# Attention pieces in one written-out sequence instead of ready lists with a table of priorities

## The chip, the cores and the metric

The kernel runs on one core of a Trainium2 chip. The metric is the device time of one execution in microseconds (us), the median of several runs. TensorE (PE) does the matmuls and the transposes; VectorE (DVE), ScalarE (ACT) and GpSimd (POOL) work on whole tiles; SyncE (SP) starts most of the transfers.

## What is computed

Sixteen heads of attention (2 batches, 8 heads, 1152 positions, 64 numbers each), in which neighbouring queries are averaged first, feed two MLPs, one behind the other.

```python
q_pool = q.reshape(B, H, S // 2, 2, D).mean(axis=3)
scores = scale * np.matmul(q_pool, k.transpose(0, 1, 3, 2))
scores = scores - np.max(scores, axis=-1, keepdims=True)
attn = np.exp(scores)
attn = attn / (np.sum(attn, axis=-1, keepdims=True) + 1e-09)
x = np.matmul(attn, v)
...
g = x @ w_gate
silu = g * (1.0 / (1.0 + np.exp(-g)))
x = (silu * (x @ w_val)) @ w_out
...
h = x @ w_in
g = np.maximum(h, 0.0) + alpha * np.minimum(h, 0.0)
out = g @ w_out
```

Between attention and the first MLP (512 to 1536 to 512) the heads are put side by side, 1152 rows of 512 numbers; the second MLP is 512 to 2048 to 512. All inputs are fp32. The kernel keeps each factor of a product as a high and a low part and multiplies three times: high by high, high by low, low by high.

## The kernel before

The kernel is written as a **plan**. Each step is one call of `add`: the engine (or two to choose from, the second in `also`), a duration from a formula for its size, what it reads and writes, the buffers and PSUM banks that it holds, and a function that writes its instructions. `plan.run` (called in L1128) puts the 2222 steps in one sequence, `plan.emit` writes their instructions in that sequence, and each engine executes its own in order. So the sequence sets the order on every engine, and with it who waits for whom.

**What sets the order.** `run` plays the kernel through as a list of events. Each engine has a ready list, sorted by priorities from the table `KNOB`: one set of numbers each for scores, minima, exponentials, transposes, evacuations and V blocks (`qk`, `mn`, `exp`, `t`, `ev`, `v`), with other sets for the first and the last pair. PE's list has two surcharges, `stay` for a step of another tile shape and `alt` for a change between scores and transposes. A step is bound to a free slot of its buffers' classes; PSUM has eight banks. While PE has nothing to do early in the plan, `run` inserts small filling matmuls (`idle`, L354). The durations (`mm`, `act`, `dve`, `gp`) are formulas of the size; a table load of ACT is in none of them.

**Attention** goes by eight pairs of heads, p0 to p7, each of 576 averaged queries: four units of 128 for both heads (`two`) and one corner of the last 64 of either head (`corner`).
- Scores: a unit is cut into three runs of 384 keys, six matmuls a cut (L719); the corner has nine matmuls in all (L738). For the first two units of p0 they are made of unsplit fp32 queries ("raw"). The sums of neighbouring queries are L662 on DVE; the queries of a whole pair are summed and split by L648 and L649 on POOL and L650 on DVE, and for the corner by L678 on POOL.
- DVE reads each cut from its bank and carries the running minimum on (L687 the first cut, L689 the others).
- ACT makes the exponentials of 1152 numbers a row and their sum (L693).
- PE transposes them, sixteen blocks at a time (L762), and the last column of blocks apart, four or two at a time (L776). ACT (L752) or DVE (L753) moves the result out of PSUM.
- V blocks (L795): the first 256 queries of a pair are one block, the other 320 a second one, each of 36 matmuls in the trace.
- The inverses of the sums go through a POOL, a DVE, a PE (L809) and an ACT step (L812) and transfers, and `finish` multiplies by them.

**The MLPs.** A third of the tokens has plain products: `contract` (L894), twelve matmuls of 384 columns. The others go by seven products in place of eight (L906, six matmuls each; DVE adds their results in L912). The Silu of the gate is L962 on ACT, its product with the value L967 on DVE. L1037 and L1071 are the second matrices of the MLPs. The weights come as 64-bit words, of which ACT (L504), DVE (L505 to L507) and POOL or DVE (L523, L524) make fp32; the high part is then split off on ACT or POOL (L485, L486), the low part on DVE or POOL (L477, L478). The MLP's bank class `b` may take four of the eight banks while attention still runs. The first plain products of the gate need tokens of the first four pairs alone, so they may stand among the steps of the last pair.

## Time and profile before

| | us |
|---|---|
| median of 3 runs | 604.35 (604.27 to 604.91) |
| the profiled execution | 604.31 |
| its span, first to last instruction | 602.5 |
| PE busy | 597.4 |
| DVE busy | 521.9 |
| ACT busy | 363.7 |
| POOL busy | 171.0 |

The profile is of one execution. The ends of PE's matmuls are modelled, so a short wait can hide in its busy time; distances between the starts of groups show it. PEld is the load of the stationary tile, and PE's waits are booked there with their releasers. A line is that of a step's instruction, so L693 is every exponential of every pair. In time, attention lasts to about 197 us, and the MLPs take the rest.

### The profile page before, as it was taken

The numbers are of one execution on the slowest core, as the hardware profiler recorded it, in microseconds if no ns is written. First come the engines' busy times: TensorE is split into PE (matmuls) and PEld (weight loads), VectorE is DVE, ScalarE is ACT, GpSimd is POOL, SyncE is SP. The second block draws the span as 40 slices with busy tenths as digits, with TensorE's granted clock in tenths as the row PEclk, the third lists the DMA queues.
The fourth block names the chain that finished last, engine by engine and source line by source line (L and its number), as shares of the span: only waits on it lengthen the run. The fifth ranks groups of instructions, "written<-read, shape, count | busy, mean of one in ns | idle before, by whom it ended". The sixth has DMA issues, their size and how long they took to land.

```text
span 602.5 us, 12214 instructions
## 1 busy us (share of the span) xinstructions
PE 597.4 (99%) x4762; PEld 532.7 (88%) x4762; DVE 521.9 (87%) x1059; ACT 363.7 (60%) x616; POOL 171.0 (28%) x187
## 2 busy tenths in 40 slices
PE   8999999999999999999999999999999999999997
PEld 5877877877877999999999999999999989989986
DVE  6998898899989899999589999889999999988552
ACT  6898888978999655555346434446575654544320
POOL 4663433523275222113320210456110300230000
PEclk9999999999999999999999999999999999999999
DMA  6342331330321313243303223121212313110012
GB/s 208 109 140 66 115 101 61 120 101 22 112 92 29 133 70 140 71 154 133 133 1 139 98 112 141 71 71 70 71 70 96 132 54 140 70 71 1 0 62 97
DMA packets 17914, 55.36 MB, mean 92 GB/s; under 512 B 2808, under 2 KB 4288, under 8 KB 17856
## 3 DMA queue, kind: packets, MB, share of 16 engines
q1 hardware_dynamic: 17568, 54.19, 25.7%
q8 instruction: 37, 0.61, 0.4%
q10 hardware_dynamic: 288, 0.39, 0.2%
q14 instruction: 21, 0.17, 0.1%
HBM read 52.17 MB, written 2.40 MB: 91 GB/s over the span
## 4 chain that ended last, share of the span: by engine, by line
PE 95%; DVE 2%; ACT 1%; issue 1%; POOL 0%; DVEq 0%; ACTq 0%
PE bank L906 24%; PE bank L1071 16%; PE bank L894 14%; PE bank L1037 12%; PE bank L795 11%; PE bank L719 8%; PE bank L762 5%; PE bank L738 2%; PE bank L776 1%; ACT wide L693 1%; DVE wide L689 1%; PE bank L354 1%; DVE wide L687 0%; DVE magnitudes L506 0%; PE bank L809 0%
## 5 line engine op out<-in xcount | busy, mean ns | idle before, releaser
L906 PE MATMUL bank<-fed,weights 128*128 128x384 f32 x600 | 114.2, 336 | 0.0
L523 POOL TENSOR_TENSOR magnitudes<-magnitudes 128x256 f32<-128x256 f32 x61 | 52.3, 873 | 217.1 <-DVE magnitudes L507 176.4
L906 PEld LDWEIGHTS bank<-fed,weights 128*128 128x128 f32 x600 | 105.6, 188 | 0.7 <-DVE plain L912 0.2
L1071 PE MATMUL bank<-wide,turned 128*128 128x512 f32 (+1 forms) x444 | 101.8, 384 | 0.0
L1071 PEld LDWEIGHTS bank<-wide,turned 128*128 128x128 f32 x444 | 81.6, 188 | 15.4
L693 ACT ACTIVATE wide<-wide,stats 128x1152 f32<-128x1152 f32 x63 | 78.8, 1252 | 21.2 <-DVE wide L689 20.9
L894 PE MATMUL bank<-x,weights 128*128 128x384 f32 x480 | 88.6, 337 | 0.0
L894 PEld LDWEIGHTS bank<-x,weights 128*128 128x128 f32 x480 | 83.8, 188 | 1.6 <-issue 0.7
L1037 PE MATMUL bank<-turned,wide 128*128 128x384 f32 x432 | 76.6, 334 | 0.0
L1037 PEld LDWEIGHTS bank<-turned,wide 128*128 128x128 f32 x432 | 75.1, 188 | 0.0
L689 DVE TENSOR_SCALAR_CACHE_REDUCE wide<-bank,stats 128x384 f32<-128x384 f32 x126 | 72.6, 613 | 1.0
L795 PE MATMUL bank<-turned,plain 128*64 128x320 f32 (+1 forms) x576 | 73.4, 409 | 0.0
L912 DVE TENSOR_TENSOR plain<-bank,plain 128x384 f32<-128x384 f32 x100 | 55.0, 550 | 13.0 <-PE bank L906 11.6
L795 PEld LDWEIGHTS bank<-turned,plain 128*64 128x64 f32 x576 | 39.9, 137 | 29.3 <-issue 2.5
L752 ACT ACTIVATE turned<-bank 128x512 f32<-128x512 f32 (+2 forms) x120 | 58.3, 555 | 4.7 <-PE bank L762 2.1
L719 PE MATMUL bank<-fed 64*128 64x384 f32 x540 | 58.0, 348 | 0.3 <-ACT plain L812 0.2
L477 DVE TENSOR_TENSOR weights<-magnitudes,weights 128x1024 fp32r<-128x1024 f32 x37 | 45.8, 1255 | 4.7 <-POOL weights L486 3.4
L906 PE MATMUL bank<-early,weights 128*128 128x384 f32 x240 | 48.5, 336 | 0.0
L719 PEld LDWEIGHTS bank<-fed 64*128 64x128 f32 x540 | 45.7, 186 | 1.4 <-ACT plain L812 0.5
L485 ACT ACTIVATE weights<-magnitudes 128x1024 fp32r<-128x1024 f32 x32 | 33.8, 1056 | 20.2 <-DVE magnitudes L507 10.4
L504 ACT ACTIVATE magnitudes<-plain 128x1024 f32<-128x1024 f32 x32 | 36.5, 1143 | 10.9 <-DVE weights L477 5.6
L953 ACT ACTIVATE turned<-plain,signs 128x384 fp32r<-128x384 f32 x48 | 28.5, 615 | 23.7 <-DVE plain L1007 23.6
(101 smaller groups left out, 877.0 us busy)
## 6 DMA issues: line engine op xcount, KB each, us to landing
plain<-in_w_out SPq DMA_DIRECT2D x28, 512.0 KB, 4.2
plain<-in_w_in SPq DMA_DIRECT2D x16, 512.0 KB, 3.2
plain<-in_w_gate SPq DMA_DIRECT2D x10, 512.0 KB, 3.3
plain<-in_w_val SPq DMA_DIRECT2D x10, 512.0 KB
plain<-in_vt SPq DMA_DIRECT2D x8, 576.0 KB, 5.3
plain<-in_qt SPq DMA_DIRECT2D x7, 576.0 KB, 3.7
plain<-in_kt SPq DMA_DIRECT2D x7, 576.0 KB, 3.6
out<-plain SPq DMA_DIRECT2D x8, 256.0 KB, 3.2
```

The costliest lines, as they stand in the source:

```text
L477: ways = [(DVE, dve(w), lambda: nc.vector.tensor_tensor(dst(), src(), hi().bitcast(F32), ALU.subtract), True), (POOL, gp2(w), lambda: nc.g ...
L523: ways = [(POOL, gp2(2 * P), lambda a=a, b=b, op=op, n=n: nc.gpsimd.tensor_tensor(U(n), a(), b(), op), True), (DVE, dve(2 * P), lambda a=a ...
L689: go = lambda: nc.vector.tensor_scalar(e.ap[:, js], src(), scale, m(i - 1), ALU.mult, ALU.min, accum_out=m(i))
L693: add(ACT, act(S, True, True), lambda: nc.scalar.activation(e.ap, e.ap, AF.Exp, bias=st.ap[:, 2:3], scale=-1.0, accum_out=x.sums.ap[:, n:n ...
L719: nc.tensor.matmul(s[j].ap[:, :CUT], l(half), r(half, js), start=a == 0, stop=a == len(terms) - 1)
L752: ACT, act(cols), lambda: nc.scalar.activation(to(), src(), AF.Copy), at + turn("ev", p, n), ts, [key], ts + [et],
L795: nc.tensor.matmul(acc.ap[half, :n], x.vn.ap[:, (j * NK + kc) * D:(j * NK + kc) * D + D], b.ap[:, (j * NK + kc) * n:(j * NK + kc) * n + n] ...
L894: nc.tensor.matmul(acc.ap[:, :TB], l, x0[:, r, c], start=c == 0 and a == 0, stop=c == KC - 1 and a == 2)
L906: nc.tensor.matmul(bank_.ap[:, :TB], l, seven(xb, k, c, r), start=first and c == 0 and n == 0, stop=c == 1 and n == 2, skip_group_check=no ...
L912: add(DVE, dve(TB), lambda: nc.vector.tensor_tensor(dst.ap, a.ap[:, :TB], b.ap, ALU.add), prio, [a] + ([b] if b is not dst else []), [dst] ...
L1037: nc.tensor.matmul(acc.ap[:, :TB], l[:, os_], r, start=n == 0 and m == 0, stop=n == len(g) - 1 and m == 2)
L1071: nc.tensor.matmul(acc.ap[:, :width], l, r[:, cols], start=n == 0 and m == 0, stop=n == len(g) - 1 and m == 2)
```

## The change

`run` no longer chooses. It takes a list of codes, `ORDER` (twice a step's number, plus one for its second engine), and places one step after the other as the list has them. The formulas are left for the choice of banks and buffers and for the number of filling matmuls. `_spot`, `_bind` and `room` go as methods, the numbers in `KNOB` are others, and in the kernel's function all lines move by 10 (L352 is L362). The diff, cut to its core; `ORDER` has 2222 codes, and one row of it is shown:

```diff
-KNOB = dict(hold_pe=0.0251, hold_act=0.2853, hold_dve=0.2093, hold_pool=13.0018, stay=9.7412, ramp=-6.5151, last=-0.69, 
...
+KNOB = dict(hold_pe=0.0169, hold_act=0.2895, hold_dve=0.1806, hold_pool=26.6713, stay=25.5753, ramp=-6.5151, last=-0.69, 
...
+ORDER = """
+8 20 10 48 50 24 12 54 34 14 39 52 26 56 60 16 22 40 18 28 30 98 62 66 58 64 86 68 88 90 42 92 70 72 94 82 84 76 32 154 44 100 46 96 36 74 79 130 102 132
...
+    def run(self, codes):
+
+        free = {PE: self.first, ACT: 0.0, DVE: 0.0, POOL: 1.7, SP: 0.6}
+        moved, port = 2.15, 0.0
+        mode, turned, valued = "rows", False, False
+        owner, binds, order = {}, {}, []
+        before = {}
+        for t in self.tasks:
+            for a in t.after:
+                before.setdefault(a, []).append(t)
+
+        def room(s, at):
+            gone = [owner[c] for c in s.cells if c in owner]
+            if any(b.users for b in gone) or any(self.classes[o]["open"] for o in s.after):
+                return None
+            until = max([b.until for b in gone], default=0.0)
+            return (0, -until) if until <= at else (1, until)
+
+        for code in codes:
+            t = self.tasks[code // 2]
+            w = t.way = t.ways[code % 2]
+            e = w.eng
+            ready = 0.0
+            for d in before.get(t, ()):
+                f = d.way.eng
+                ready = max(ready, d.done + (0.0 if f == e == PE and not d.extra else 0.216 if f == e == DVE else self.LAT[f] + (0.05 if f == POOL != e else 0.0)))
+            idle = [i for i in range(8) if ("ps", i) not in owner or (not owner["ps", i].users and owner["ps", i].until <= free[PE])]
+            at = max(free[e], ready)
+            for i, b in enumerate(t.bufs):
+                if b.slot is None:
+                    spots = [(room(s, at), k, s) for k, s in enumerate(self.classes[b.cls]["slots"])]
+                    _, _, b.slot = min(x[:2] + (x[2],) for x in spots if x[0] is not None)
+                    ready = max([ready] + [owner[c].until for c in b.slot.cells if c in owner])
+                    for c in b.slot.cells:
+                        owner[c] = b
+                    cells = sorted(c[1] for c in b.slot.cells if c[0] == "ps")
+                    if cells:
+                        binds.setdefault(t, []).extend((c, b.cls in "vmb" or (j == 1 if len(cells) == 2 else i == 1)) for j, c in enumerate(cells))
+            start = max(free[e], ready, port if w.port and e == DVE else 0.0)
+            end = start + w.dur
+            if e == PE:
+                if mode == "rows" and not valued and idle:
+                    order += [idle] * int((start - free[e]) / 0.058)
+                if start > free[e] + 1e-6:
+                    end += self.STALL
+                if t.mode != mode:
+                    end += self.TURN[mode, t.mode]
+                    mode = t.mode
+                if mode == "rows":
+                    end += 0.05 if turned and t.kind == "s" else 0.0
+                    turned = t.kind == "t"
+                valued = valued or mode == "cols"
+            if w.port:
+                end = port = max(start, port) + w.dur
+            free[e] = end
+            t.start, t.done = start, end + t.late
+            if t.extra:
+                moved = max(start + 1.25, moved) + t.extra
+                t.done = moved + 0.85
+            for b in t.bufs:
+                b.until = max(b.until, t.done + self.LAT[e])
+                b.users -= 1
+                if not b.users:
+                    self.classes[b.cls]["open"] -= 1
+            order.append(t)
+        self.end = max(t.done for t in self.tasks)
+        self.order = []
+        top = [False] * 8
+        for k in reversed(order):
+            if isinstance(k, list):
+                able = [i for i in k if top[i]]
+                if able:
+                    self.order.append(lambda i=able[-1]: self.idle(i))
+            self.order.append(k.way.emit)
+            for i, low in binds.get(k, ()):
+        self.order.reverse()
...
-    plan.run({PE: K["hold_pe"], ACT: K["hold_act"], DVE: K["hold_dve"], POOL: K["hold_pool"], SP: 0.0}, K["stay"], K["alt"])
+    plan.run([int(c) for c in ORDER.split()])
```

In the program PE has 5 filling matmuls of 128 columns where it had 35; its other matmuls are the same ones. 94 steps are on another engine: two of the first splits of keys go from ACT and DVE to POOL, some ten evacuations net from DVE to ACT, three weight splits from ACT to POOL. ACT has six table loads where it had two. The order differs most at the start and in the last two pairs; PE's last 176 groups are the same in both.

**The start, DVE.** Before, from its first instruction (`bank` is PSUM, `wide` the scores of a unit, `fed` the split queries and keys, `stats` the minima):

```order
L429 MEMSET plain 128x256
L662 TENSOR_TENSOR plain<-plain 128x128
L642 TENSOR_TENSOR fed<-plain,fed 128x384
L687 TENSOR_SCALAR wide_133,stats<-bank 128x384
L689 TENSOR_SCALAR wide_133,stats<-bank,stats 128x384
L687 TENSOR_SCALAR wide_133,stats<-bank 128x384
L689 TENSOR_SCALAR wide_133,stats<-bank,stats 128x384
L662 TENSOR_TENSOR plain<-plain 128x128
L689 TENSOR_SCALAR wide_133,stats<-bank,stats 128x384 x2
L687 TENSOR_SCALAR wide_133,stats<-bank 128x384 x2
L689 TENSOR_SCALAR wide_133,stats<-bank,stats 128x384
L650 SCALAR_TENSOR_TENSOR fed<-plain,fed 128x576
```

After, from its first instruction:

```order
L439 MEMSET plain 128x256
L672 TENSOR_TENSOR plain<-plain 128x128
L697 TENSOR_SCALAR wide_120,stats<-bank 128x384 x2
L699 TENSOR_SCALAR wide_120,stats<-bank,stats 128x384
L672 TENSOR_TENSOR plain<-plain 128x128
L699 TENSOR_SCALAR wide_120,stats<-bank,stats 128x384 x3
L697 TENSOR_SCALAR wide_120,stats<-bank 128x384 x2
L699 TENSOR_SCALAR wide_120,stats<-bank,stats 128x384
L660 SCALAR_TENSOR_TENSOR fed<-plain,fed 128x576
L699 TENSOR_SCALAR wide_120,stats<-bank,stats 128x384 x2
```

The second sum of queries (L662, now L672) stands behind three minima and not four, the split of keys (L642) is gone from here, and the split of queries (L650, now L660) stands behind nine minima as before.

**The start, PE.** Before, from the last raw scores (`plain` at L719) to the first V block:

```order
L719 MATMUL bank<-plain 128x384 x4
L762 MATMUL bank<-plain,wide_133 128x64 x16
L719 MATMUL bank<-plain 128x384 x2
L762 MATMUL bank<-plain,wide_133 128x64 x16
L776 MATMUL bank<-plain,wide_133 128x64 x4
L738 MATMUL bank<-fed 128x384 x9
L762 MATMUL bank<-plain,wide_133 128x64 x16
L719 MATMUL bank<-fed 128x384 x6
L762 MATMUL bank<-plain,wide_133 128x64 x16
L776 MATMUL bank<-plain,wide_133 128x64 x4
L719 MATMUL bank<-fed 128x384 x30
L795 MATMUL bank<-turned_207,plain 64x256 x18
```

After, to the first V block; ahead of it stand twelve raw scores in a row, sixteen transposes, four of the last column and two filling matmuls:

```order
L772 MATMUL bank<-plain,wide_120 128x64 x16
L729 MATMUL bank<-fed 128x384 x6
L748 MATMUL bank<-fed 128x384 x9
L772 MATMUL bank<-plain,wide_120 128x64 x16
L729 MATMUL bank<-fed 128x384 x6
L772 MATMUL bank<-plain,wide_120 128x64 x16
L729 MATMUL bank<-fed 128x384 x6
L786 MATMUL bank<-plain,wide_120 128x64 x4
L729 MATMUL bank<-fed 128x384 x18
L805 MATMUL bank<-turned_170,plain 64x256 x18
```

Six split scores stand ahead of the corner, and the 30 scores ahead of the V block are parted by transposes.

**Pair 7, ACT.** Before, the last exponentials (L693) and the first Silu (L962):

```order
L693 ACTIVATE plain,allsums<-plain,stats 128x1152
L485 ACTIVATE fed<-plain 128x384
L693 ACTIVATE wide_133,allsums<-wide_133,stats 128x1152 x2
L752 ACTIVATE turned_207<-bank 128x8x64 x2
L752 ACTIVATE turned_207<-bank 128x2x2x64
L798 ACTIVATE plain<-bank 128x256
L752 ACTIVATE turned_207<-bank 128x8x64
L812 ACTIVATE plain<-bank 9x128
L752 ACTIVATE turned_207<-bank 128x8x64 x2
L485 ACTIVATE weights_2710<-magnitudes 128x1024
L962 ACT_TABLE_LOAD
L962 ACTIVATE plain<-bank 128x384
```

After, behind the first two exponentials of pair 7:

```order
L972 ACT_TABLE_LOAD
L972 ACTIVATE plain<-bank 128x384
L703 ACT_TABLE_LOAD
L703 ACTIVATE plain,allsums<-plain,stats 128x1152
L762 ACTIVATE turned_170<-bank 128x8x64
L703 ACTIVATE wide_120,allsums<-wide_120,stats 128x1152
L972 ACT_TABLE_LOAD
L972 ACTIVATE plain<-bank 128x384
L762 ACTIVATE turned_170<-bank 128x8x64
L762 ACTIVATE turned_170<-bank 128x2x2x64
L762 ACTIVATE turned_170<-bank 128x8x64 x5
L703 ACT_TABLE_LOAD
```

Two Silus (now L972) stand between exponentials (now L703), and each change of function has a table load ahead of it.

**Pair 7, PE.** Before, from the V block of pair 7's first 256 queries:

```order
L795 MATMUL bank<-turned_207,plain 64x256 x18
L776 MATMUL bank<-plain,wide_133 128x64 x2
L776 MATMUL bank<-plain 128x64 x2
L762 MATMUL bank<-plain,wide_133 128x64 x16
L762 MATMUL bank<-plain 128x64 x16
L776 MATMUL bank<-plain,wide_133 128x64 x4
L762 MATMUL bank<-plain,wide_133 128x64 x32
L809 MATMUL bank<-plain 128x64 x2
L894 MATMUL bank<-x_67,weights_2710 128x384 x12
L795 MATMUL bank<-turned_207,plain 64x320 x18
L894 MATMUL bank<-x_67,weights_2710 128x384 x36
```

After, inside pair 7 (L904 is the gate's plain product, L729, L748, L772 and L786 are scores, corner, transposes and last-column transposes); behind it come 30 scores, then the V block of 320 queries of pair 6 and that of 256 of pair 7 in a row:

```order
L904 MATMUL bank<-x_67,weights_2393 128x384 x12
L748 MATMUL bank<-fed 128x384 x6
L772 MATMUL bank<-plain,wide_120 128x64 x16
L786 MATMUL bank<-plain,wide_120 128x64 x4
L904 MATMUL bank<-x_67,weights_2393 128x384 x12
L748 MATMUL bank<-fed 128x384 x3
L772 MATMUL bank<-plain,wide_120 128x64 x16
L786 MATMUL bank<-plain,wide_120 128x64 x2
L786 MATMUL bank<-plain 128x64 x2
L772 MATMUL bank<-plain,wide_120 128x64 x16
L729 MATMUL bank<-fed 128x384 x6
L772 MATMUL bank<-plain 128x64 x16
```

Two plain products of the gate stand among the transposes of pair 7, and the V block of 320 queries of pair 6 stands behind all scores of pair 7.

## Rows read from the trace of the kernel before

**Rows 1.** The page: busy time by engine, clock in 40 slices, chain by engine.

```profile
PE 597.4 (99%) x4762; PEld 532.7 (88%) x4762; DVE 521.9 (87%) x1059; ACT 363.7 (60%) x616; POOL 171.0 (28%) x187
...
PEclk9999999999999999999999999999999999999999
...
PE 95%; DVE 2%; ACT 1%; issue 1%; POOL 0%; DVEq 0%; ACTq 0%
```

**Rows 2.** Windows: stretch, busy us of PE, PEld, DVE, ACT, POOL, clock, DMA.

```profile
150.00:200.00 50.00, 49.67 (x637) 37.46 (x634) 45.65 (x118) 45.39 (x81) 22.97 (x24) 1.00 0.23 79
...
240.00:260.00 20.00, 20.00 (x115) 19.74 (x114) 19.72 (x31) 9.62 (x17) 2.36 (x3) 1.00 0.23 77
```

**Rows 3.** PE's waits: line, releaser, total us, times, longest.

```profile
PEld bank L776 <- ACT wide L693: 2.3, 6, 0.4
...
PEld bank L906 <- DVE plain L912: 0.6, 3, 0.3
```

**Rows 4.** Timeline of PE at the start: start us, duration us, engine, line, operation, count.

```profile
7.27 1.72 PE L354 MATMUL bank<-plain 64*128 64x128 bf16 x28
...
10.18 0.71 PE L762 MATMUL bank<-plain,wide 64*128 64x64 f32 x16
...
12.85 1.99 PE L738 MATMUL bank<-fed 128*128 128x384 f32 x9 [0.27 <-POOL fed L678]
...
16.55 3.17 PE L719 MATMUL bank<-fed 64*128 64x384 f32 x30
19.65 4.11 PE L795 MATMUL bank<-turned,plain 128*64 128x256 f32 x36
```

**Rows 5.** Timeline of DVE, ACT and POOL at the start.

```profile
7.72 0.61 DVE L689 TENSOR_SCALAR_CACHE_REDUCE wide<-bank,stats 128x384 f32<-128x384 f32 x1
...
8.26 0.29 DVE L662 TENSOR_TENSOR plain<-plain 128x128 f32<-128x128 f32 x1
...
11.29 0.75 DVE L650 SCALAR_TENSOR_TENSOR fed<-plain,fed 128x576 fp32r<-128x576 f32 x1
...
9.87 1.26 ACT L693 ACTIVATE wide<-wide,stats 128x1152 f32<-128x1152 f32 x1
...
12.13 0.67 POOL L678 TENSOR_SCALAR fed<-fed 64x128 fp32r<-64x128 f32 x2 [0.98 <-DVE fed L650]
```

**Rows 6.** Timeline of PE, pairs 5 to 7.

```profile
139.47 0.34 PE L776 MATMUL bank<-plain,wide 64*128 64x64 f32 x4
...
165.83 0.88 PE L762 MATMUL bank<-plain,wide 64*128 64x64 f32 x16
...
166.95 0.82 PE L719 MATMUL bank<-fed 64*128 64x384 f32 x6
...
167.75 0.79 PE L738 MATMUL bank<-fed 128*128 128x384 f32 x3
168.69 0.80 PE L719 MATMUL bank<-fed 64*128 64x384 f32 x6 [0.15 <-ACT plain L812]
...
186.82 0.27 PE L776 MATMUL bank<-plain,wide 64*128 64x64 f32 x2
...
189.40 0.22 PE L809 MATMUL bank<-plain 64*128 64x64 f32 x2
...
196.86 6.51 PE L894 MATMUL bank<-x,weights 128*128 128x384 f32 x36
```

**Rows 7.** Groups of ACT by form: count, busy us, mean ns.

```profile
L752 ACT ACTIVATE turned<-bank 128x512 f32<-128x512 f32 x98 | 52.6, 600 | 2.3 <-PE bank L762 2.1
...
L962 ACT ACT_TABLE_LOAD x1 | 1.3, 1283 | 0.0
```

**Rows 8.** Timeline of ACT, pair 5's exponentials and the first Silu.

```profile
145.17 1.26 ACT L693 ACTIVATE wide<-wide,stats 128x1152 f32<-128x1152 f32 x1 [1.36 <-DVE wide L689]
...
191.87 1.28 ACT L962 ACT_TABLE_LOAD   x1
193.16 0.49 ACT L962 ACTIVATE plain<-bank 128x384 f32<-128x384 f32 x1
```

149 lines of the change are left out of this document (9 added, 140 removed), and 68 rows, old and new, of the table ORDER.

## The prediction

> **What bounds the kernel now.** I read the busy times, the clock row and the chain of waits first. PE works 597.4 of 602.5 us, the clock row is 9 in all forty slices, and 95% of the chain that ended last is PE [rows 1]. So the kernel costs what its matmuls cost, and a new order can only take away PE's waits, its idle start, or add to them. There is little to take: 602.5 - 597.4 = 5.1 us without PE work, most of it ahead of its first instruction and behind its last. The busy time hides some waits, since the ends of matmuls are modelled, so I also compared distances between starts.
>
> Second, the windows: where is another engine near the bound, so that a moved instruction of its own reaches PE? Two stretches stand out [rows 2]. In 150 to 200 us ACT works 45.39 and DVE 45.65 of 50 us; in 240 to 260 DVE works 19.72 of 20. Elsewhere there is air: over the whole span ACT is at 60%. Third, PE's own waits by releaser: the largest with a name are the last-column transposes behind the exponentials, 2.3 us in 6 places, and the seventh products behind the sums, 0.6 us in 3 [rows 3].
>
> The span lies 604.31 - 602.5 = 1.8 us under the time of its execution; the median of the runs is 604.35. I add the sum to 604.35.
>
> **Startup.** In before PE has only filling matmuls from 7.27 to almost 9, because the scores of the second unit need the second sum of queries, which stands on DVE behind four minima, at 8.26 [rows 4, 5]. After has it behind three, so one spacing of minima earlier: 8.26 - 7.72 = 0.54 us. This alone is not what PE gains: the corner scores go through DVE's L650 (11.29) and two POOL splits (12.13, until 12.80) and start at 12.85 [rows 4, 5]. After keeps that chain, with L660 again behind six further minima. What it gains is that six scores stand ahead of the corner, no longer behind it, while PE would wait: one cut, 0.55 us (five cuts without waits take 5 x 0.55 = 2.74). The 30 scores at 16.55 took 3.10 us to the first value matmul at 19.65, 0.36 more than that [rows 4]; after places them in three runs between transposes and later minima, so I let this wait go. A new one comes: the four last-column transposes now stand in PE's queue ahead of the second sixteen, and need the second exponential, which ended at 11.13 in before (9.87 + 1.26) and hardly sooner now; until 11.2 PE then has nothing, but neither had it the corner's inputs. Sum: -0.55 - 0.36 = **-0.95 us**. Bounds: -1.3 if the earlier query sum also carries the L650 chain forward (two thirds of its 0.54), -0.3 if the 30 scores keep their wait and nearly half of the cut is lost.
>
> **Filling matmuls.** Thirty go. They ran where PE had nothing else, so they cost nothing now and give nothing back, as long as the granted clock stays where it is.
>
> **Pairs 6 and 7, PE's waits.** From 158 to 197 us I compared starts with clean runs (0.49 us for sixteen transposes, 0.17 for four, 0.55 for a cut). The row of 165.83 takes 1.12 to the scores at 166.95, 0.46 too much; three corner matmuls from 167.75 take 0.94 to 168.69, 0.22 too much; 64 transposes and eight last-column ones from 186.82 take 2.58 to 189.40, some 0.3 too much [rows 6]. With three smaller ones the stretch waits 1.3 us. The new order has other neighbours here, so these go: **-1.3**. It sets pair 6's V block of 320 and pair 7's of 256 in a row and all of the last transposes behind them, whose last evacuations nothing covers: **+0.5**, between 0.3 (one evacuation at its spacing of 0.5 us, half covered) and 0.9. One change of tile shape less on PE: -0.1.
>
> **Pairs 6 and 7, the table loads.** This is what I expect to decide. The Silu of the gate and the exponential are different functions of ACT, and the program loads a table where one follows the other: in before twice, at the start and at 191.87, for 1.28 us each [rows 7, 8]. The new sequence sets two gate products (L904) with their Silus between the exponentials of pair 7. ACT's program now holds six loads: four more, 4 x 1.283 = 5.13 us, on the engine that had 4.6 us of air in fifty. How much PE sees I walked through, with t = 0 at the end of pair 6's V block of 256.
> - Without the loads, PE's queue up to the V block of pair 6's other 320 queries, which now follows all scores of pair 7, is eight sixteens of transposes (3.9 us), 16 last-column ones (0.7), twelve cuts of scores (6.6), nine corner matmuls (2.0 [rows 4]) and 24 gate matmuls (4.3: 36 took 6.5 at 196.86 [rows 6]): 17.5, with the turns between tile shapes 17.6 us. ACT's evacuations then stay ahead of it.
> - In pair 5 the first exponential behind the V block began 5.70 us after it (139.47 to 145.17) [rows 6, 8]; in the new queue the minima that it needs come at the same distance or up to 0.65 later. From there ACT's queue is two exponentials (2 x 1.26), load 1.28, Silu 0.49, load 1.28, exponential 1.26, evacuation 0.5 (0.6 less the overlap with what follows), exponential 1.26, load 1.28, Silu 0.49 [rows 7, 8]: 10.4 us, so the second Silu ends at 16.1 to 16.7.
> - The second Silu reads the PSUM bank that the next sixteen transposes behind its gate product is to write. From there to the V block PE has two sixteens, four single ones, six scores, a sixteen and thirty scores: 0.49 + 0.2 + 0.49 + 0.6 + 0.49 + 2.74 = 5.0 us. The V block starts at 21.1 to 21.7 where it could start at 17.6.
> So **+3.5 to +4.1, taken +3.7**. The fourth load lies under the two V blocks (4.11 us for the narrower alone [rows 4]). Bounds: 0, if the banks come free sooner than I read, and 5.13, if all four stand on the path.
>
> The Trainium skill ("ScalarE: Activation LUTs", What ACT_TABLE_LOAD costs) gives 1283 ns for the load and some 1380 ns for a drain besides, 2.66 us a switch, and speaks against this order (Table sets: the hidden batching unit: all of one set together). The trace has the 1283 ns but not the drain at 191.87: the Silu starts 1.29 us after the load's start.
>
> **The rest.** In the middle pairs the PE order is nearly the old one; fewer changes between scores and transposes, -0.2 (0 to -0.4). Where the MLP starts, half of the wait of the seventh products on sums [rows 3] goes: -0.3 (0 to -0.6); DVE has a microsecond less work there, POOL three more of the free kind. PE's last 176 groups are the same in both programs: 0.
>
> **Sum:** -0.95 - 1.3 + 0.5 - 0.1 + 3.7 - 0.2 - 0.3 = +1.35. The forecast is 604.35 + 1.35 = **605.7 us**, slower.
>
> **Rivals.**
> 1. *The loads are hidden.* For it: PE's queue has 24 gate matmuls, 4.2 us, that need nothing of ACT, and the transposes have other banks. Then 605.7 - 3.7 = 602.0. Against it: ACT is the engine behind which PE's named waits stand [rows 3]. It decides the sign as soon as less than 1.1 us of the loads is left. Chance 0.17.
> 2. *Half shown.* One of the two switch pairs falls where PE has its gate matmuls, one delays it by a load and a Silu, 1.8 us: 603.8, no change that can be told. Chance 0.30.
> 3. *Each switch costs more than its load.* If the exponential that follows a load starts late by as much again (no row of before has Exp behind a Silu; the only row is Silu behind a copy [rows 8]), up to four times 1.3 us come on top, three of them on the path: 605.7 + 3.9 = 609.6. Chance 0.06.
> The figure of the Trainium skill's page above, 1380 ns of drain a switch, would give 609.8 by three.
> 4. *The filling matmuls were needed.* PE now stands idle at some 7.2 to 8.0 and 10.4 to 11.2. If the granted clock fell from 2.4 to 1.2 GHz there, the scores of the second unit, 1.2 us from the filling's end at 8.99 to the first transposes at 10.18 [rows 4], would take twice as long, and those sixteen transposes too: +1.7, 607.4. Against it: the clock row stands at its top from the first slice [rows 1], though PE's work there was thin. Chance 0.07.
> 5. *The chain at the MLP's start misses its cover.* The last V block's division, splits and sums run on DVE, which is full from 240 us [rows 2]; if they come late by one sum more, +1: 606.7. Inside my range for the forecast, whose chance is 0.40 with it.
>
> **How the numbers follow.** A measurement of this kernel tells some 0.2% from no change, 1.2 us: faster is under 603.15, slower over 605.55. The forecast's own range is 604.4 to 607.0 by the bounds of its terms; a third of its 0.40 falls below 605.55, but cases 3 and 4 and the upper end of 2 come on the slow side. Faster: case 1 and the lower end of 2, 0.17 + 0.09 = 0.26. Slower: 0.26 of the forecast, 0.06 + 0.07, 0.03 of case 2, 0.42. The rest, 0.32, is the same. The range leaves out the lower half of case 1, case 3 and the far end of case 4: 602.2 to 607.8.
>
> **What would show it.** Six table loads on ACT, four of them between 164 and 185 us; PE's waits there on ACT's exponential and Silu lines, together 3 to 4 us, at the last-column transposes, at the three corner matmuls and at the sixteens behind them. The first value matmul at 18.7 rather than 19.65. The clock row still full. Waits of the evacuations after the two V blocks of pair 7 of half a microsecond. And MLP stretches as long as before. I am wrong if PE runs through pair 7 with no named wait (case 1), if an exponential starts late behind its load (case 3), or if the first slices of the clock row drop (case 4).

## The result and the profile after

The changed kernel took 608.05 us (median of 6 runs, 606.8 to 609.37), the kernel before 604.31 in the runs beside it (603.64 to 604.91). The ratio is 1.0064, with a 95% interval of 1.0047 to 1.0081: slower by 0.64%, and 0.25 us above the top of the predicted range. The profiled execution took 607.29 us, its span 605.5, 3.0 more than before.

The page of the changed kernel: busy time by engine, the granted clock in 40 slices, the chain by engine, to be held against [rows 1].

```profile
PE 595.8 (98%) x4732; PEld 531.3 (88%) x4732; DVE 521.4 (86%) x1054; ACT 363.9 (60%) x622; POOL 173.1 (29%) x190
...
PEclk9999999999999999999999999999999999999999
...
PE 87%; DVE 7%; ACT 3%; issue 2%; POOL 0%; DVEq 0%; ACTq 0%; POOLq 0%
```

PE works less (thirty filling matmuls are gone) and the span is longer: 9.7 us without PE work in place of 5.1. In the chain DVE and ACT now have 10% where they had 3%.

The same windows as [rows 2]: the length, then busy us of PE, PEld, DVE, ACT, POOL, then clock and DMA.

```profile
150.00:200.00 50.00, 46.07 (x609) 35.74 (x607) 40.28 (x111) 44.93 (x79) 27.91 (x28) 1.00 0.13 47
...
240.00:260.00 20.00, 19.81 (x114) 19.49 (x113) 19.84 (x30) 12.34 (x20) 2.33 (x3) 1.00 0.31 107
```

In the stretch of pairs 6 and 7 PE works 46.07 us where it worked 49.67. ACT is at 44.93 where it was at 45.39, so it is no busier in this window, but four table loads, 5.13 us, now stand in it where one stood.

PE's waits from 160 to 206 us: line, releaser, total us, times, longest.

```profile
PEld bank L772 <- ACT plain L972: 1.6, 1, 1.6
PEld bank L819 <- DVE turned L763: 1.1, 1, 1.1
PEld bank L786 <- ACT plain L972: 0.9, 1, 0.9
PEld bank L748 <- ACT turned L762: 0.8, 1, 0.8
```

Two of the four stand behind L972, the Silu of the gate, whose first one stood behind all exponentials before, at 193.16 [rows 8]. ACT's rows of the same stretch in order of time: table loads, Silus, exponentials (L703), and the high split that stands behind the fourth load (L495):

```profile
170.12 1.28 ACT L972 ACT_TABLE_LOAD   x1
171.42 0.49 ACT L972 ACTIVATE plain<-bank 128x384 f32<-128x384 f32 x1
171.93 1.28 ACT L703 ACT_TABLE_LOAD   x1
173.22 1.26 ACT L703 ACTIVATE plain<-plain,stats 128x1152 f32<-128x1152 f32 x1
...
176.31 1.28 ACT L972 ACT_TABLE_LOAD   x1
177.60 0.49 ACT L972 ACTIVATE plain<-bank 128x384 f32<-128x384 f32 x1
...
181.57 1.28 ACT L703 ACT_TABLE_LOAD   x1
182.86 1.25 ACT L703 ACTIVATE wide<-wide,stats 128x1152 f32<-128x1152 f32 x1
...
184.12 0.92 ACT L495 ACTIVATE fed<-plain 128x384 fp32r<-128x384 f32 x2
186.59 1.26 ACT L703 ACTIVATE plain<-plain,stats 128x1152 f32<-128x1152 f32 x1 [1.55 <-DVE plain L699]
```

And PE's: the first group behind pair 6's V block of 256 queries (161.34), the groups that wait, and the V blocks behind them (L805).

```profile
161.34 0.34 PE L786 MATMUL bank<-plain,wide 64*128 64x64 f32 x4
...
171.96 0.34 PE L786 MATMUL bank<-plain,wide 64*128 64x64 f32 x4 [0.72 <-ACT plain L972]
...
175.11 0.79 PE L748 MATMUL bank<-fed 128*128 128x384 f32 x3 [0.52 <-ACT turned L762]
...
178.15 0.71 PE L772 MATMUL bank<-plain,wide 64*128 64x64 f32 x16 [1.46 <-ACT plain L972]
...
182.58 8.95 PE L805 MATMUL bank<-turned,plain 128*64 128x320 f32 x72
...
193.29 0.28 PE L819 MATMUL bank<-plain 64*128 64x64 f32 x2 [0.94 <-DVE turned L763]
...
197.58 5.07 PE L805 MATMUL bank<-turned,plain 128*64 128x320 f32 x36
```

From 161.34 to the V block of pair 6's other queries at 182.58 it takes 21.24 us; the walk of the prediction had 21.1 to 21.7. The three waits lie where they were expected: 0.72 at the last-column transposes, 0.52 at the three corner matmuls, 1.46 at the sixteens behind the second Silu; together 2.70, where 3 to 4 were expected. What was not expected is the wait of 0.94 at 193.29, behind the two V blocks.

To see in time where the 3.0 us arise, I took the start of the same matmul in both traces and in those of the experiments below. V0 is the first V block of pair 0 (19.65 in before), V6 that of pair 6 (158.42), M48, M200 and M300 are the matmuls behind the first 48, 200 and 300 of the lines L894 and L906 (203.21, 230.03 and 247.49), the end is PE's last matmul (598.96). Each number is the trace's start less that of before. V6 in before:

```profile
158.42 4.11 PE L795 MATMUL bank<-turned,plain 128*64 128x256 f32 x36
```

| | V0 | V6 | M48 | M200 | M300 | end |
|---|---|---|---|---|---|---|
| changed kernel | -0.56 | -1.12 | +2.64 | +2.25 | +3.13 | +3.00 |
| e1_exp | -0.98 | -1.55 | -2.61 | -2.99 | -2.15 | -2.28 |
| e6_one | -0.56 | -1.07 | -0.16 | -0.54 | +0.31 | +0.18 |
| e7_dve | -0.58 | -1.15 | +1.50 | +1.12 | +1.97 | +1.87 |
| e5_copy | -0.55 | -0.85 | -1.86 | -2.24 | -1.40 | -1.51 |
| e15_copy2 | -0.89 | -1.47 | -2.50 | -2.88 | -2.02 | -2.12 |
| e9_best | -0.98 | -1.56 | -2.60 | -2.99 | -1.84 | -1.54 |
| e3_head | -0.95 | -1.58 | -0.74 | -0.73 | -0.73 | -0.09 |
| e14_late2 | -0.57 | -0.84 | +4.54 | +4.16 | +5.00 | +4.90 |
| e13_latefill | -0.84 | -1.41 | +1.79 | +1.41 | +2.24 | +2.02 |

### The profile page after: what moved, and what is told of

Same layout as the page of the kernel before. It is cut to its first block, busy times and chain, and to the rows that moved or that the text cites. A ratio compares the mean times of both kernels' runs of the same rounds, so it can differ in the third digit from the quotient of the medians.

```text
span 605.5 us, 12134 instructions
## 1 busy us (share of the span) xinstructions
PE 595.8 (98%) x4732; PEld 531.3 (88%) x4732; DVE 521.4 (86%) x1054; ACT 363.9 (60%) x622; POOL 173.1 (29%) x190
## 4 chain that ended last, share of the span: by engine, by line
PE 87%; DVE 7%; ACT 3%; issue 2%; POOL 0%; DVEq 0%; ACTq 0%; POOLq 0%
PE bank L916 20%; PE bank L1081 16%; PE bank L1047 12%; PE bank L904 11%; PE bank L805 10%; PE bank L729 8%; PE bank L772 5%; PE bank L748 2%; DVE plain L922 1%; DVE wide L699 1%; PE bank L786 1%; DVE weights L487 1%; ACT wide L703 1%; DVE magnitudes L517 1%; PE bank L364 1%
## 5 line engine op out<-in xcount | busy, mean ns | idle before, releaser
L533 POOL TENSOR_TENSOR magnitudes<-magnitudes 128x256 f32<-128x256 f32 x58 | 50.6, 885 | 203.1 <-DVE magnitudes L517 155.0
L904 PE MATMUL bank<-x,weights 128*128 128x384 f32 x480 | 89.1, 337 | 0.0
L904 PEld LDWEIGHTS bank<-x,weights 128*128 128x128 f32 x480 | 83.9, 188 | 1.8 <-issue 0.7
L703 ACT ACTIVATE wide<-wide,stats 128x1152 f32<-128x1152 f32 x58 | 72.5, 1255 | 17.6 <-DVE wide L699 15.2
L699 DVE TENSOR_SCALAR_CACHE_REDUCE wide<-bank,stats 128x384 f32<-128x384 f32 x116 | 68.8, 615 | 5.2 <-PE bank L748 1.4
L805 PE MATMUL bank<-turned,plain 128*64 128x320 f32 (+1 forms) x576 | 73.2, 408 | 0.0
L762 ACT ACTIVATE turned<-bank 128x512 f32<-128x512 f32 (+2 forms) x128 | 61.7, 551 | 7.1 <-PE bank L772 4.8
L805 PEld LDWEIGHTS bank<-turned,plain 128*64 128x64 f32 x576 | 40.0, 137 | 29.4 <-DVE wide L699 1.3
L729 PE MATMUL bank<-fed 64*128 64x384 f32 x540 | 56.7, 347 | 0.0
L487 DVE TENSOR_TENSOR weights<-magnitudes,weights 128x1024 fp32r<-128x1024 f32 x38 | 46.3, 1230 | 0.5 <-POOL weights L496 0.4
L729 PEld LDWEIGHTS bank<-fed 64*128 64x128 f32 x540 | 45.4, 186 | 1.0
L916 PEld LDWEIGHTS bank<-early,weights 128*128 128x128 f32 x240 | 42.3, 188 | 0.2
```

The source lines that it names most:

```text
L487: ways = [(DVE, dve(w), lambda: nc.vector.tensor_tensor(dst(), src(), hi().bitcast(F32), ALU.subtract), True), (POOL, gp2(w), lambda: nc.g ...
L533: ways = [(POOL, gp2(2 * P), lambda a=a, b=b, op=op, n=n: nc.gpsimd.tensor_tensor(U(n), a(), b(), op), True), (DVE, dve(2 * P), lambda a=a ...
L699: go = lambda: nc.vector.tensor_scalar(e.ap[:, js], src(), scale, m(i - 1), ALU.mult, ALU.min, accum_out=m(i))
L703: add(ACT, act(S, True, True), lambda: nc.scalar.activation(e.ap, e.ap, AF.Exp, bias=st.ap[:, 2:3], scale=-1.0, accum_out=x.sums.ap[:, n:n ...
L729: nc.tensor.matmul(s[j].ap[:, :CUT], l(half), r(half, js), start=a == 0, stop=a == len(terms) - 1)
L762: ACT, act(cols), lambda: nc.scalar.activation(to(), src(), AF.Copy), at + turn("ev", p, n), ts, [key], ts + [et],
```

## The experiments

The variants' lines have numbers 2 to 11 higher than those of the changed kernel. "Before" stands for the runs of the kernel before beside each.

### The table loads

**e1_exp: the loads away, all else as it is.**

```diff
+        bends.append(0)
+        fn = AF.Exp if len(bends) <= 2 else AF.Silu
-        add(ACT, act(TB, inside), lambda: nc.scalar.activation(dst.ap, src.ap[:, :TB], AF.Silu), prio, ...
+        add(ACT, act(TB, inside), lambda: nc.scalar.activation(dst.ap, src.ap[:, :TB], fn), prio, ...
```

> The changed kernel with one edit: the first two Silus (the two inside pair 7) are exponentials, so that ACT needs no table load there; every order, tile and bank is as in the changed kernel. The gate of a third of the tokens in the first two blocks is therefore another function. Theory A (the four extra loads cost PE some 3.7 us at pair 7): two loads are left, no wait of PE on the gate's Silu line, pair 6's V block of 320 queries starts some 17.6 us behind the block of 256 in place of 21.2, and the time falls by 3.3 to 3.9 us against the changed kernel (span of a run at full clock near 602.0). Rival B (the gate products in pair 7 cost by their banks and their place, not by the loads): less than 1 us comes back. On the spread of the changed kernel's runs (606.8 to 609.4, mean clock 0.996 to 1.000): if it comes from PE's waits at pair 7, all runs here have a clock of 1.000 and lie within 0.6 us; if it comes from the start, it stays.

602.30 us (602.01 to 603.53) beside 604.15 of before, ratio 0.9975 (0.9963 to 0.9986). PE in pairs 6 and 7:

```profile
160.91 0.34 PE L788 MATMUL bank<-plain,wide 64*128 64x64 f32 x4
...
178.78 8.95 PE L807 MATMUL bank<-turned,plain 128*64 128x320 f32 x72
187.66 0.40 PE L788 MATMUL bank<-plain,wide 64*128 64x64 f32 x6
...
192.34 5.07 PE L807 MATMUL bank<-turned,plain 128*64 128x320 f32 x36
```

From 160.91 to 178.78 it is 17.87 us, where the prediction's walk without loads had 17.6 and the changed kernel has 21.24: three loads cost PE 3.4 us there. But 187.66 to 192.34 is 4.68 us, and the same stretch of the changed kernel, 191.46 to 197.58, took 6.12: another 1.4 us go with the fourth load. From V6 to M48 the loads cost 3.76 - (-1.06) = 4.82 us of their 5.13, more than the 3.3 to 3.9 expected. The medians lie 5.75 apart, or 4.92 against the changed kernel's runs in e12_again (607.22), in which the clock did not fall. Rival B falls. The clocks here are 0.999 and 1.000, yet the runs spread over 1.5 us and not 0.6, so the clock is not the only thing that spreads them.

**e6_one: one of the two pairs of loads.**

```diff
-        fn = AF.Exp if len(bends) <= 2 else AF.Silu
+        fn = AF.Exp if len(bends) == 2 else AF.Silu
```

> The changed kernel with only the second of the two Silus in pair 7 made an exponential (the gate of one tile is another function), so two of the four extra loads are gone, those around the second Silu. Theory A2 (each load stands on the path with its own length): 602.3 + 2 x 1.28, some 604.9 at full clock; PE's waits of 0.7 us at the four last-column transposes and 0.5 at the three corner matmuls stay, the one of 1.5 behind them and the one of 1.1 ahead of the last transposes go. Rival H (the loads cost by their sum, the first two are hidden by the gate products): 603.0 or less.

604.92 us (604.01 to 606.16), before 604.70. From V6 to M48 it takes +0.91 where e1_exp takes -1.06 and the changed kernel +3.76: the first two loads cost 1.97, the other two 2.85, for 2.57 of either pair's own length. Both pairs reach the path, as Theory A2 has it, and rival H falls. The waits of 0.7 and 0.5 us are still there in its trace, the other two are gone.

**e7_dve: how the fourth load reaches PE.** DVE's rows in the changed kernel: the low split L487 waits 1.36 us for ACT's high split, which stands behind the fourth load (ACT's 184.12 above), and minima (L699) are queued behind it; the exponential at 186.59 waits for those.

```profile
184.65 0.56 DVE L487 TENSOR_TENSOR fed<-plain,fed 128x384 fp32r<-128x384 f32 x1 [1.36 <-ACT fed L495]
185.13 0.61 DVE L699 TENSOR_SCALAR_CACHE_REDUCE plain<-bank,stats 128x384 f32<-128x384 f32 x1
```

In `ORDER` the split's code goes behind the last minimum of pair 7:

```diff
-... 1898 1900 1842 ... 1622 1850 1854 ...
+... 1898 1842 ... 1622 1850 1900 1854 ...
```

> The changed kernel with one DVE step moved: the low split of a part of pair 7's tokens, which waits for ACT's high split behind the fourth load, goes behind the last minimum of pair 7. Theory K (the fourth load reaches the path through this step, with five minima queued behind it): 1.0 to 1.4 us come back, all between pair 7's first and last V block: 606.7 to 607.1. Rival L (the exponentials behind the fourth load are late by themselves): less than 0.4 us.

607.41 us (606.17 to 607.93), 0.64 less in the median than the changed kernel's first measurement and no less than its second (e12_again below, 607.22). In the trace V6 to M48 takes 2.65 against 3.76, so 1.1 us are back; the wait at the last transposes is gone, and 0.5 has come up between the two V blocks, where a wait of 0.31 has a name:

```profile
187.94 4.11 PE L807 MATMUL bank<-turned,plain 128*64 128x256 f32 x36 [0.31 <-DVE wide L701]
```

In one trace the mechanism is shown for the larger part; the runs' spread is too wide for their medians to confirm its size. The hole of 1.55 us in ACT's queue at 186.59 is not the load's work: e5_copy below, without the load, has it too (1.56), but earlier, and there PE is still covered. The load pushes it past the cover.

**e4_late: the gate products away from pair 7.** The codes of both products and their Silus go ahead of pair 7's last V block.

```diff
-... 1744 1960 1962 1748 ... 1974 1964 1746 ... 1718 1966 1762 ... 1648 1888 ...
+... 1744 1748 ... 1974 1746 ... 1718 1762 ... 1648 1960 1962 1964 1966 1888 ...
```

> The changed kernel with four steps moved: the two plain gate products and their Silus stand ahead of pair 7's last V block, behind the last exponential, as one of them did in the kernel before. Two table loads in place of six. Theory A: 3.7 us come back at pair 7, and less than 1 is lost since PE has no gate products to do while ACT makes exponentials: 604.5 to 605.5. Rival F (the gate products were the cover of pair 7's exponentials): their 4.3 us stand behind attention and the same waits come back without them: 607 or more.

608.98 us (607.79 to 609.23), before 604.15. With two loads in place of six it is slower than the changed kernel: rival F. Pair 7's transposes now wait for exponentials and minima that the gate products had covered; the longest wait is 2.13 us. In the trace the clock falls within that wait, and the mean clock is below 1 in each execution (0.993 to 0.997). PE's row and the windows of one us (PE, PEld, DVE, ACT, POOL, clock):

```profile
174.81 0.37 PE L788 MATMUL bank<-plain,wide 64*128 64x64 f32 x2 [2.13 <-DVE wide L701]
```

```profile
173.00:174.00 1.00, 0.00 (x0) 0.00 (x0) 1.00 (x3) 1.00 (x2) 0.85 (x2) 1.00 0.00 0
174.00:175.00 1.00, 0.18 (x4) 0.22 (x6) 0.81 (x4) 0.90 (x3) 0.98 (x1) 0.73 0.00 0
175.00:176.00 1.00, 1.00 (x22) 1.00 (x20) 1.00 (x3) 0.39 (x1) 0.00 (x0) 0.50 0.00 0
...
177.00:178.00 1.00, 1.00 (x20) 1.00 (x18) 0.75 (x3) 0.23 (x1) 0.00 (x0) 0.56 0.00 0
178.00:179.00 1.00, 1.00 (x16) 1.00 (x15) 0.64 (x3) 0.95 (x2) 0.00 (x0) 1.00 0.00 0
```

So the gate products are well placed in pair 7. It was their Silus that were not.

**e5_copy: the products stay, the Silus go.**

```diff
+        if len(bends) <= 2:
+            add(ACT, act(TB), lambda: nc.scalar.activation(dst.ap, src.ap[:, :TB], AF.Copy), prio, [src], [dst], [src, dst])
+            add(ACT, act(TB, True), lambda: nc.scalar.activation(dst.ap, dst.ap, AF.Silu), prio, [], [dst], [dst])
+            return dst
```

> The whole result, without the extra loads: as the changed kernel, but in pair 7 ACT only copies the two gate products out of PSUM, and their Silus are made from those copies ahead of the evacuation of pair 7's last V block, where the MLP's first table load comes anyway. Two ACT steps of 0.5 us more, four loads fewer. Theory A (the loads, not the gate products, cost the time): as the kernel with exponentials in place of the two Silus, 602.3, at most 602.9, faster than before by 0.2 to 0.3%. Rival G (the later Silus hold up the gate's products with the values): 603.5 or more, with waits of DVE on the gate's Silu line at the MLP's start.

602.52 us (601.98 to 605.95), before 604.70, ratio 0.9975 (0.9962 to 0.9987). This kernel is faster than both: 0.25% against before by the ratio, whose interval is clear of 1, and 0.8 to 0.9% against the changed kernel by the medians, which are of other chips. From V6 to M48 it takes -1.01, as e1_exp does (-1.06). Rival G falls. One of its twelve runs had a mean clock of 0.997 and took 605.95. On another chip, as e15_copy2:

> The kernel with copies in place of the two early Silus once more, on another chip: 602.0 to 602.8 us and faster than before by 0.2 to 0.3% if its gain is the kernel's and not the chip's.

602.53 us (602.16 to 604.36), before 604.19, ratio 0.9976 (0.9964 to 0.9987).

### The clock

**e2_fill: filling matmuls back at the start.**

```diff
+FILL = {49: 15, 41: 13}
...
+                order += [(idle,)] * FILL.get(t.n, 0)
```

> The changed kernel with 28 filling matmuls of 128 columns put back, fifteen ahead of the second unit's raw scores and thirteen ahead of the four last-column transposes, the two places at the start where PE stands idle. Theory C (without fillers the granted clock falls at the start in some executions): all runs have a clock of 1.000, they lie within 0.6 us of each other, and the median falls by 0.7 to 1.5 us to about 607. Rival D (the clock falls elsewhere, or fillers only delay the scores): the clocks still lie between 0.996 and 1.000 and the median stays at 608 or rises by up to 0.5.

607.80 us (607.23 to 608.77), clocks 0.996 to 1.000. Theory C falls: the start needs no fillers. But its profiled execution was one in which the clock fell, and it shows where, right behind PE's waits in pair 7 (windows as above):

```profile
174.00:178.00 4.00, 2.40 (x28) 1.70 (x26) 2.53 (x7) 3.97 (x7) 1.04 (x2) 1.00 0.00 0
178.00:182.00 4.00, 3.62 (x44) 3.53 (x46) 1.05 (x4) 2.95 (x7) 0.00 (x0) 0.59 0.00 0
182.00:186.00 4.00, 4.00 (x40) 2.90 (x40) 2.75 (x11) 3.97 (x7) 0.00 (x0) 0.98 0.01 4
```

From V6 to M48 this trace takes 4.8 us where the changed kernel's, at full clock, takes 3.8: the fall costs 1.0 us there.

**e8_fillp7: filling matmuls in pair 7.**

```diff
+FILL = {862: (14, 3), 875: (26, 7)}
```

> The changed kernel with 40 filling matmuls of 128 columns in pair 7: 14 ahead of the four last-column transposes, 26 ahead of the sixteen transposes that wait for the second Silu. No load goes. Theory M (PE's waits at pair 7 let the granted clock fall in a part of the executions): the clock is 1.000 in all runs, they lie within 0.8 us, and the median is 607.0 to 607.5, that is 0.5 to 1 less. Rival N (the fall has nothing to do with these waits): clocks of 0.994 to 0.997 stay in about half of the runs, median 608 or more.

607.23 us (606.94 to 607.43), five clocks of 1.000. As Theory M has it; but on that chip the clock of e7_dve, without fillers, hardly fell either, so this pair does not decide. At full clock the fillers neither cost nor save: V6 to M48 takes 3.74 in this trace.

**e12_again: the changed kernel on another chip.**

> The changed kernel once more, to see its runs on the chip of these experiments. By Theory M (PE's waits at pair 7 let the clock fall in a part of the executions) the runs at a clock of 1.000 lie at 606.8 to 608.1 and those at 0.994 to 0.997 a microsecond or more above.

607.22 us (606.83 to 608.69), clocks 0.999 to 1.000, before 604.59; ratio 1.0048 (1.0033 to 1.0064). Here the clock did not fall, and one run at 608.69 has full clock all the same: a spread of 1.9 us that the clock does not explain, which the other kernels have too (before, beside it: 603.59 to 605.98).

**e14_late2 and e13_latefill: the decision**, on e4_late, whose clock fell each time.

> The same kernel without the fillers, once more, for the comparison on one chip: clocks of 0.993 to 0.997 in all runs and 608 to 609 us, whatever the theory.

```diff
+FILL = {862: (14, 5), 881: (38, 4)}
```

> The kernel with the gate products moved out of pair 7 (whose clock was below 1.000 in each of its executions: the granted clock was 0.50 from 175 to 177, behind 2.1 us in which PE waited), with 52 filling matmuls ahead of the two groups of last-column transposes at which PE waits. Theory M (PE's waits let the clock fall, and the half clock behind them costs time): the clock is 1.000 in all runs, and the time falls by 1 to 1.7 us against the same kernel without fillers on the same chip. Rival N (the wait costs its own length and no more, the clock falls with or without work): clocks of 0.993 to 0.997 stay and the time is the same within 0.4 us.

e14_late2: 609.43 us (609.14 to 611.42), clocks 0.993 and 0.994. e13_latefill: 606.31 us (606.24 to 607.92), clocks 0.999 and 1.000. The windows of both, first without, then with the fillers:

```profile
176.00:177.00 1.00, 1.00 (x11) 0.93 (x9) 0.59 (x1) 0.84 (x2) 0.00 (x0) 0.50 0.00 0
...
178.00:180.00 2.00, 2.00 (x16) 2.00 (x16) 1.12 (x5) 1.92 (x4) 0.00 (x0) 0.50 0.00 0
```

```profile
176.00:177.00 1.00, 1.00 (x19) 0.93 (x15) 1.00 (x6) 0.98 (x3) 0.00 (x0) 1.00 0.00 0
...
178.00:180.00 2.00, 2.00 (x22) 1.20 (x20) 2.00 (x10) 1.82 (x4) 0.00 (x0) 1.00 0.00 0
```

Work that serves nothing but to fill a wait is worth 3.1 us in the median; in the traces 2.2 between V6 and M48, while 0.6 lies ahead of V6, where the two programs are the same. The wait was lost anyway; what the fillers save is the time behind it at 1.2 GHz, and they save more than expected. On this kernel Theory M holds.

### The parts of the sequence

**e3_head: the new sequence up to pair 6's V block, then the old order.**

```python
pre = AFTER[:AFTER.index(V6)]
ORDER = pre + [c for c in BEFORE if c // 2 not in {x // 2 for x in pre}]
```

> The first part of the change alone: the written-out sequence up to pair 6's V block of 256 queries, and behind it all other steps in the order of the kernel before (so no exponential behind a Silu, two table loads). Theory A with the two traces (that V block started 1.1 us earlier in the changed kernel): faster than before by some 1.1 us, 603.2 at full clock; by Theory C with runs up to 1.5 us above that, at a mean clock below 1.000. Rival E (the new head of the sequence brings nothing that lasts): 604.3 or more at full clock.

604.91 us (604.16 to 605.46), before 604.15; ratio 1.0012 (1.0003 to 1.0021). Theory A missed: V6 is 1.58 earlier, but half of it is lost by the next V block (170.95, where before has 171.74), and 0.64 at 264 us in one wait on DVE's gate product. Why pair 6 loses it stays open; 0.6 of it lies at one cut of scores at 162.04, for which DVE's and ACT's evacuations (L765, L764) are named. In the second stretch DVE was busy 21.85 of 22 us in the trace of before as well. The wait, and that window of before:

```profile
PEld bank L1049 <- DVE plain L979: 0.8, 1, 0.8
```

```profile
258.00:280.00 22.00, 22.00 (x128) 22.00 (x127) 21.85 (x32) 13.41 (x24) 3.50 (x4) 1.00 0.39 144
```

**e10_tail: the other way round.** The same two lines with before and after exchanged.

> The other part of the change alone: the order of the kernel before up to pair 6's V block of 256 queries, and behind it all other steps in the order of the written-out sequence, with its six table loads (and 4 filling matmuls of 128 columns where the kernel before has 35). Theory A with the traces: the part from that V block on lost 4.1 us in the changed kernel, so before + 4.1 = 608.5 at full clock, more where the clock falls in pair 7. If it comes out under 607, the head of the sequence bears a part of the loss.

616.11 us (615.32 to 616.35), clocks 0.991 and 0.992. A miss by 7.6 us: at the seam PE waits 1.87 us for minima and goes on at half clock (0.80 over 158 to 170, 0.75 to 174), again in pair 7 (0.62 over 186 to 190). It says nothing of the tail; two halves of different sequences don't add up.

**e9_best: the MLP's two waits.** The kernels with the new tail lose 0.83 to 0.92 us from M200 to M300 (e10_tail 0.57), in two waits; in the changed kernel:

```profile
PEld bank L916 <- DVE plain L922: 1.0, 2, 0.5
```

In e9_best, made from e5_copy, two DVE steps of the weights go behind the sums that PE waits for, L518 by three rows and L517 by five:

```diff
-L518 SCALAR_TENSOR_TENSOR magnitudes<-plain,magnitudes 128x1024
 L924 TENSOR_TENSOR plain<-bank,plain 128x384 x3
+L518 SCALAR_TENSOR_TENSOR magnitudes<-plain,magnitudes 128x1024
...
-L517 TENSOR_SCALAR magnitudes<-magnitudes 128x1024
...
 L924 TENSOR_TENSOR plain<-bank,plain 128x384 x3
+L517 TENSOR_SCALAR magnitudes<-magnitudes 128x1024
```

> The kernel with copies in place of the two early Silus, and two DVE steps of the weights (L518 and L517 there) set behind the three sums that PE waits for, in the MLP's first part. In the changed kernel and in all its variants PE loses some 0.85 us between its 200th and 300th MLP matmul, in two waits of 0.5 us on the seventh products' sums, which the kernel before doesn't have. Theory P (those two DVE steps cause them): both waits go, 0.7 to 0.9 us come back, 601.7 at the fast end. Rival Q (DVE is full there, so the wait moves to a later sum): less than 0.3 us.

603.20 us (602.76 to 604.44), before 604.59, ratio 0.9977 (0.9968 to 0.9986). The median is 0.7 above e5_copy's, but the ratio is not to be told from e5_copy's 0.9975. The trace has lost 0.7 against e5_copy's: M200 to M300 takes +1.15, 0.3 more, and 0.4 more goes behind M300. The waits are three on the sums and one on the weights that now come late:

```profile
PEld bank L918 <- DVE plain L924: 0.8, 3, 0.4
PEld bank L906 <- DVE weights L489: 0.5, 1, 0.5
```

The gain that Theory P foretold is not there. But the trial does not show that a full DVE passes the wait on, as rival Q has it: the third sum, behind which L518 now stands, is not ready, and DVE itself stands idle for it.

```profile
234.50 0.56 DVE L924 TENSOR_TENSOR plain<-bank,plain 128x384 f32<-128x384 f32 x1 [1.42 <-PE bank L918]
```

So the step was moved too far back, and whether a smaller move would help was not tried.

**e11_hyb: e5_copy up to pair 7's last V block, then the old order.**

> The kernel with copies in place of the two early Silus, up to and with pair 7's last V block, and behind it all other steps in the order of the kernel before. If the MLP's loss of 0.85 us is the order's own, it goes: 601.7. If DVE is the bound there (as in the kernel with the head alone, which lost 0.8 us on DVE's gate product at 266 us), PE's lead of 1.9 us is given back at some point between 240 and 270 us, whatever the order: 603.5 or more.

603.38 us (602.92 to 604.46), before 604.59. M48 is at -2.07, and the end at -0.73: it loses 0.62 between M48 and M200 on a copy of ACT, and 0.72 behind M300 on DVE's gate product (at 263.6 us), as e3_head did; from M200 to M300 it loses nothing. The loss is less than expected if DVE were the only bound (603.5 or more) and more than if it were not; it stays open how much of the new tail's 0.85 a better order could save.

## Why the prediction was wrong

The direction and the place were right, the size was not: 3.0 us in the trace against +1.35, and 3.7 in the medians. Two steps failed: the fourth load was given no price, and PE's waits in pair 7 were priced at their length alone, without the clock behind them. A smaller term, the MLP's, had the wrong sign. By the prediction's own terms, forecast against trace:

| step | forecast | measured |
|---|---|---|
| start, up to V0 | -0.95 | -0.56 |
| middle pairs, V0 to V6 | -0.2 | -0.56 |
| pairs 6 and 7 without the loads | -0.9 | -1.06 (e1_exp, V6 to M48) |
| the table loads | +3.7 | +4.82 (changed kernel less e1_exp) |
| the MLP | -0.3 | +0.36 (M48 to the end) |
| sum | +1.35 | +3.00 |

- **What bounds the kernel.** Right, and with it the choice of windows: all that decided lies in 158 to 250 us.
- **The start.** Within its bounds. In fourteen traces of kernels that have the new start, V0 lies 0.24 to 1.01 us earlier than in [rows 4], so a part of this is the execution's; e10_tail, with the old order here, lies 0.42 earlier too. The wait at the four last-column transposes came as told (11.36), and the corner at 13.00 and not sooner than before:

```profile
11.36 0.34 PE L786 MATMUL bank<-plain,wide 64*128 64x64 f32 x4 [0.62 <-DVE wide L699]
...
13.00 1.83 PE L748 MATMUL bank<-fed 128*128 128x384 f32 x9
...
19.09 4.11 PE L805 MATMUL bank<-turned,plain 128*64 128x256 f32 x36
```

- **The middle pairs.** -0.56 here, and 0.27 to 0.63 us less in all fourteen traces, where 0 to 0.4 was given; no run takes this term apart.
- **The filling matmuls.** Right that they cost and give nothing (e2_fill); rival 4 did not happen where it was placed.
- **PE's waits in pairs 6 and 7.** Right to 0.2 us as a sum; its three parts were not measured apart.
- **The table loads: the step that failed.** "The fourth load lies under the two V blocks" ("+3.5 to +4.1, taken +3.7") counted only ACT's own work against the cover of the two V blocks. ACT's next step behind that load was a split for DVE, DVE had five minima queued behind its half of the split, and the last exponentials need those: the load left ACT's queue through DVE's (e7_dve). I had looked at the first three loads by walking through ACT's and PE's queues, and at the fourth by adding durations on one. The first three came to 3.4 against 3.7, with some luck: the second Silu ended at the late end of its range (16.75, where 16.1 to 16.7 was given), and PE took 4.5 us from there and not 5.0, because a sixteen and the four single ones ran ahead of the wait. The bound of 5.13 was given, and the 4.82 of all four lies near it.
- **The MLP.** Here I read DVE's row of [rows 2], named it full, and still forecast a gain, because DVE has a microsecond less work in all. PE got two new waits of 0.5 us. A smaller total does not say where a sum stands behind a weight step. Which order would spare the waits stays open: e9_best only moved them, and e11_hyb, with the old order from there on, lost 1.34 us at other places.
- **The clock: a cause that was put in the wrong place.** Rival 4 had the fall at the start, where the fillers were taken away. In e2_fill's trace it came in pair 7, behind PE's new wait of 1.5 us; the changed kernel's own trace is of an execution at full clock. Three of the first six runs had a mean clock of 0.996 or 0.997 and took 608.0 to 609.4, the others 606.8 to 608.1. The three at full clock have a median of 607.29 and the runs of e12_again one of 607.22, both within the range; with the fall the median is 608.05. e5_copy, without the loads, had one such run in twelve, so these waits may not be the only place; where it fell there no trace shows.
- **Rival 3** (more than the load for each switch) didn't happen: the exponential behind the load of 171.93 starts at 173.22, 1.29 us later, as Silu did in [rows 8]. The Trainium skill ("ScalarE: Activation LUTs", What ACT_TABLE_LOAD costs) adds a drain of some 1380 ns to the load's 1283; the load agrees to the nanosecond and no run here shows the drain. Its rule to batch the activations by table set (Table sets: the hidden batching unit) agrees with these runs: doing that, with a copy in place of each early Silu, is what made the faster kernel (e5_copy).
- **Rivals 1 and 2** fell with e1_exp and e6_one.
- **Two slips of the sums.** -0.55 - 0.36 is -0.91, not -0.95, which makes the sum +1.39. And by these terms the sign turns when less than 2.35 us of the loads is left; rival 1's 1.1 us is where the gain reaches 1.2.

The gain that the new sequence does bring without the loads is 1.7 to 2.2 us by the medians, some 1.5 by the ratios, as e1_exp, e5_copy and e15_copy2 show against the runs of before beside them. What lost the time is an instruction that neither order names: the program holds it wherever a Silu follows an exponential, or an exponential a Silu.

## What to carry to other kernels

Before an order is judged, list the instructions that it adds between steps: a table load belongs to no step, and a planner without its price will mix exponentials with Silus as if it were free. Where a step falls late, follow what it releases through the queue of the next engine, and what is queued behind that, before calling it covered. And where TensorE must wait in the middle of a kernel, give the wait a second price for the clock behind it; filling matmuls are worth a trial there, not only at the start.

## What the runs showed of the hardware

- A wait of PE in the middle of a busy kernel can bring the granted clock to 0.50, the 1.2 GHz level. In the traces of e4_late and e14_late2 it fell within a wait of 2.1 us (with 0.4 and 0.7 shortly before), and PE, fully busy, went on at 0.50 for 3 us and for 5 us; the mean clock was 0.993 to 0.997 in all nine runs of this kernel. In e2_fill's trace it fell right behind a wait of 1.5 us, and in the traces of the changed kernel and e12_again it did not fall behind the same wait. With 52 small matmuls in the waits of e13_latefill it stayed at 1.00, for 3.1 us less. The Trainium skill ("TensorE: Matmul & The Clock Gate", HAM oscillation — how this bites in real kernels) tells of kernels that wait for transfers and go on cold; these traces agree, with waits of 2.1 us for minima and exponentials.
- While POOL's four sums ran, the same DVE step of the weights took 1.64 us, and 1.21 six microseconds sooner. The longer one stands right ahead of the sums for which PE waits 0.46 us at 239.59; whether its 0.43 us more make that wait was not tested:

```profile
231.35 1.21 DVE L516 SCALAR_TENSOR_TENSOR magnitudes<-plain,magnitudes 128x1024 int32<-128x1024 int32 x1
...
237.43 1.64 DVE L516 SCALAR_TENSOR_TENSOR magnitudes<-plain,magnitudes 128x1024 int32<-128x1024 int32 x1
```

```profile
235.44 5.04 POOL L533 TENSOR_TENSOR magnitudes<-magnitudes 128x256 f32<-128x256 f32 x4 [7.30 <-DVE magnitudes L517]
```
